# Moving six element-wise instructions on q from VectorE to GpSimd in an attention and MLP kernel

## The chip, the cores and the metric

The kernel runs on one core of one Trainium2 chip. The metric is the device time of one execution in microseconds (us). The kernel before takes 832.39 us, the median of 3 runs (832.22 to 834.11). The execution whose profile is read here took 833.08 us by itself; its span, from the first recorded instruction to the last, is 831.2 us.

## What is computed

Eight batches of linear attention, each with 8 heads, 576 positions and 64 features a head, feed a two-layer network:

```python
q_s = q - np.max(q, axis=-1, keepdims=True)
q_s = np.exp(q_s)
q_s = q_s / (np.sum(q_s, axis=-1, keepdims=True) + 1e-09)
k_s = k - np.max(k, axis=2, keepdims=True)
k_s = np.exp(k_s)
k_s = k_s / (np.sum(k_s, axis=2, keepdims=True) + 1e-09)
kv = np.einsum('bhsd,bhse->bhde', k_s, v)
x = np.einsum('bhsd,bhde->bhse', q_s, kv)      # then rows of 8 * 64 = 512
h = x @ w_in
sp = np.maximum(h, 0.0) + np.log1p(np.exp(-np.abs(h)))
out = (h * erf(sp)) @ w_out
```

The softmax of q is taken along the 64 features, that of k along the 576 positions. The change concerns two steps of the softmax of q: the subtraction of the maximum ahead of the exponential, and the multiplication by the reciprocal of the sum behind it.

## The kernel before, in words

**Attention.** A batch's q lies in SBUF as two tiles of 128 partitions x 1024 float32 values (`q_0` and `q_1` in the profile's and the order's names: half 0 and half 1 of the heads; 16 rows of 64 features in each partition). The last 64 positions of two batches share one tail tile of 128 x 512 (`qt`). k lies in two tiles of the same size and a tail `kt`. The function `attention(b)` emits the steps of one batch:

- `k_max` (lines 517, 518, 521) folds k to one row of maxima by `tensor_tensor` on VectorE, ending with the tail at L521. Four transposes on TensorE (`kT`, L528), a reduction on VectorE (`km`, L532) and four more transposes (`kB`, L543) bring the maxima back to all partitions, and L703 (twice) and L708 subtract them from k.
- `q_sub` takes the maxima of 16 rows (`tensor_reduce`, L464, into `q_m`, a tile with one buffer) and subtracts them (`tensor_tensor`, L465), in place.
- ScalarE takes the exponentials of k's and q's tiles (L348).
- `kv_mm` (L564) forms k times v on TensorE, `kv_norm` divides (L584 to L587).
- `q_norm` sums 16 rows (L471), adds and inverts (L473 or L475, L476) and multiplies in place (L478).
- q is then transposed on TensorE (`q_T`, L661; from batch 3 on by a DMA), copied by ScalarE (L651, L654), multiplied by kv (L679), and the product x is put into SBUF by ScalarE (L453). The PSUM tiles of q's transposes, of kT, kB, kv and of x share one pool of two banks (tag `bk`), so a transpose may have to wait until ScalarE has read an older tile.

**The network.** Tokens are cut into 12 blocks of 384, the hidden width into 4 groups of 512, which gives 48 steps n. Step n multiplies by w_in (`m`; L1036 in float32 for the first five steps, L997 in split float16 with one level of Strassen's scheme after that), takes softplus and erf on ScalarE (L348, with an activation table load ahead of each), multiplies on VectorE (L1074 or L1077), splits the result into two float16 parts (L1091, L1095) and multiplies by w_out (`M`; L1114 in float32, L1123 in float16). In the first 110 us VectorE also decodes the weights (three instructions for each piece: L213, L216, L219), and ScalarE squares them (L248) for a scale that `wscales` makes (from L257 on, with the transposes of L263 on TensorE and the reductions of L267 on VectorE). `wsplit` and `finish` split the weights and x into float16 parts (L299 on ScalarE, L300 on VectorE).

**Order.** The table ORDER and the function `pace` say in which order the steps are emitted. A list scheduler with its own cost estimates then sets the order on each engine; each engine runs its instructions strictly in that order. An instruction that is put on another engine therefore changes the order of others too. GpSimd's queue holds a few memsets (L443, L444), the loads of some weights (L187), and for batch 0 the subtraction of q's maxima (L857, four instructions of 128 x 512); SyncE's queue issues the other DMAs.

Of the kernel before, what the change touches and what calls it, by code (L numbers as in the profile page):

```python
# [55 lines left out]
def attn_moe_kernel(  # L56
# [9 lines left out]
    nc = tc.nc  # L66
# [276 lines left out]
    def act(out_, in_, func, chain=True, **kw):  # L343

        with ExitStack() as es:
            if chain and last[0] is not None:
                es.enter_context(tc.issue_after(last[0]))
            i = nc.scalar.activation(out_, in_, func, **kw)  # L348
        if chain:
            last[0] = i.ins  # L350
        return i
# [106 lines left out]
    def rows(t):  # L458
        return t.rearrange("p t h d -> p (t h) d")

    def q_sub(t, g, name):

        m = at.tile([P, g], F32, tag=f"qm{g}", bufs=1, name=f"{name}_m")
        nc.vector.tensor_reduce(m, t, axis=AX.X, op=ALU.max)  # L464
        nc.vector.tensor_tensor(  # L465
            t, t, m[:, :, None].to_broadcast([P, g, D]), op=ALU.subtract
        )

    def q_norm(t, g, name, b, o=None):
        r = at.tile([P, g], F32, tag=f"qr{g}", bufs=1, name=f"{name}_r")  # L470
        nc.vector.tensor_reduce(r, t, axis=AX.X, op=ALU.add)  # L471
        if b < E32:
            nc.vector.tensor_scalar_add(r, r, 1e-9)  # L473
        else:
            nc.vector.tensor_scalar(r, r, 1e-9, 2.0**-QS, op0=ALU.add, op1=ALU.mult)  # L475
        nc.vector.reciprocal(r, r)  # L476
        if o is None:
            nc.vector.tensor_tensor(  # L478
                t, t, r[:, :, None].to_broadcast([P, g, D]), op=ALU.mult
            )  # L480
            return
        for f in range(2):
            fs = slice(4 * f, 4 * f + 4)
            nc.vector.tensor_tensor(
                o[:, f * 2 * P:(f + 1) * 2 * P].rearrange("p (c a d) -> p a c d", c=2, a=2),
                t[:, fs].rearrange("p (a c) d -> p a c d", a=2),
                r[:, fs].rearrange("p (a c) -> p a c", a=2)[..., None].to_broadcast([P, 2, 2, D]),
                op=ALU.mult,
            )
# [22 lines left out]
    def k_max(b, ks, kt):  # L512

        kmax = asc[:, 0].rearrange("p (h d) -> p h d", h=H)
        k2 = asc[:, 1].rearrange("p (t h d) -> p t h d", t=2, h=4)
        for hf in range(2):
            nc.vector.tensor_tensor(k2, ks[hf][:, 0:2], ks[hf][:, 2:4], op=ALU.max)
            nc.vector.tensor_tensor(
                kmax[:, hf * 4:hf * 4 + 4, :], k2[:, 0], k2[:, 1], op=ALU.max
            )  # L520
        nc.vector.tensor_tensor(kmax[kt[1]], kmax[kt[1]], kt[0], op=ALU.max)  # L521
        return kmax

    def k_max_T(b, kmax):
        bk = bank(f"kT_{b}")
        km2 = hd(kmax)
        for c in range(NC4):
            nc.tensor.transpose(  # L528
                bk[:, c * P:(c + 1) * P], km2[:, c * P:(c + 1) * P], ident
            )  # L530
        km = at.tile([P, NC4], F32, tag="km", bufs=1, name=f"km_{b}")
        nc.vector.tensor_reduce(  # L532
            km, bk.rearrange("p (c s) -> p c s", c=NC4), axis=AX.X, op=ALU.max
        )
        return km
# [3 lines left out]
    def k_max_rows(b, km):  # L539

        bk = bank(f"kB_{b}")
        for c in range(NC4):
            kB[0] = nc.tensor.transpose(  # L543
                bk[:, c * P:(c + 1) * P], km[:, c:c + 1].to_broadcast([P, P]), ident
            )
        return bk.rearrange("p (h d) -> p h d", h=H)
# [97 lines left out]
    def q_turn_tail(p):  # L644
        t = q_turn(hd(bat[2 * p]["qt"]), asc[:, 0].bitcast(F16), 2)
        bat[2 * p]["qtT"] = t.rearrange("p (i c) s -> p i (c s)", i=2)
# [44 lines left out]
    def attention(b):  # L691
        d, j, p = bat[b], b % 2, b // 2
        even = bat[b - j]
        tl = slice(j * TAIL, (j + 1) * TAIL)
        ks, qs, kt = d["k"], d["q"], even["kt"][tl]
        kmax = k_max(b, ks, (kt, tl))
        yield SHARES[0]
        km = k_max_T(b, kmax)
        q_sub(rows(qs[0]), 16, f"q_{b}_0")
        yield SHARES[1]  # L700
        kb = k_max_rows(b, km)
        for hf in range(2):
            nc.vector.tensor_tensor(  # L703
                ks[hf], ks[hf],
                kb[:, None, hf * 4:hf * 4 + 4, :].to_broadcast([P, TM, 4, D]),
                op=ALU.subtract,
            )
        nc.vector.tensor_tensor(kt, kt, kb[tl], op=ALU.subtract)  # L708
        yield SHARES[2]
        q_sub(rows(qs[1]), 16, f"q_{b}_1")  # L710
        if j == 1:
            q_sub(even["qt"], H, f"qt_{p}")
        yield SHARES[3]
        for t in (*ks, kt, qs[0], qs[1], *([even["qt"]] if j == 1 else [])):
            act(t, t, AF.Exp, chain=b > 1)
        yield SHARES[4]
        kv_norm(b, 0, kv_mm(b, 0))
        if b > 1:
            d["v"].append(load_half(v, "v", b, 1))
        q_norm(rows(qs[0]), 16, f"q_{b}_0", b)  # L720
        yield SHARES[5]
        if b >= QDMA:
            q_turn_half(b, 0)
        kv_norm(b, 1, kv_mm(b, 1))
        if b + 1 < B:
            load_kv(b + 1)
        mx = kv_max(b)
        yield SHARES[6]
        kv_split(b, mx)
        yield SHARES[7]  # L730
        q_norm(rows(qs[1]), 16, f"q_{b}_1", b)
        if b >= QDMA:
            q_turn_half(b, 1)
        if j == 1:
            q_norm(even["qt"], H, f"qt_{p}", b, asc[:, 1] if b < QDMA else None)
            if b >= QDMA:
                q_turn_tail(p)
        yield SHARES[8]
        for i in ((3 * p + 1, 3 * p + 2) if j else (3 * p, 3 * p + 1)):
            while not x_free(i):  # L740
                yield 0

        def tails():
            if b < QDMA:
                bk = bank(f"qTt_{p}")
                for c in range(NC4):
                    nc.tensor.transpose(
                        bk[:, c * P:(c + 1) * P], asc[:, 1, c * P:(c + 1) * P], ident
                    )
                even["qtT"] = q_evac(b, 0, bk)  # L750
            yield SHARES[9]
            qT = even["qtT"]
            bks = [bank(f"xt_{p}_{a}") for a in range(2)]
            x = xblock(p * NBK + 1)
            for j_ in range(2):
                for hf in range(2):
                    oc = slice(hf * P + j_ * TAIL, hf * P + (j_ + 1) * TAIL)
                    qs_ = [
                        qT[:, :, (2 * hf + c) * P + j_ * TAIL:(2 * hf + c) * P + (j_ + 1) * TAIL]
                        for c in range(2)  # L760
                    ]
                    x_mm(2 * p + j_, hf, [bk[:, oc] for bk in bks], qs_)
            w = TAIL if b < E32 else P
            for a, bk in enumerate(bks):
                bk3 = bk[:, :2 * P].rearrange("p (f s) -> p f s", f=2)
                for j_ in range(P // w):
                    o = SM - T + j_ * TAIL
                    x_put(
                        bk3[:, :, j_ * TAIL:j_ * TAIL + w], x[:, a::2, o:o + w],
                        bat[j_]["sx"] if b < E32 else None,  # L770
                    )
            if b + 1 < B:
                bat[b + 1]["qt"] = load_tail(q, "qt", p + 1)
            yield SHARES[10]

        if j == 1 and b < QDMA:
            yield from tails()
        for hf in range(2):
            if hf == 1 and j == 1 and b >= QDMA:
                yield from tails()  # L780
            qTs = []
            for c in (2 * hf, 2 * hf + 1):
                qTs.append(q_T(b, c, bank(f"qT_{b}_{c}")) if b < QDMA else d["qT"][c])
                if b < QDMA and c % 2 == 1 and b + 1 < B:
                    load_q(b + 1, hf)
                yield SHARES[11]
            bks = [bank(f"x_{b}_{hf}_{a}") for a in range(2)]
            x_mm(b, hf, bks, qTs)
            if b >= QDMA and b + 1 < B:
                load_q(b + 1, hf)  # L790
            for a in range(2):
                x_split(b, 2 * hf + a, bks[a])
            if hf == 1:
                d["xdone"] = True
            yield 2 * SHARES[12]
# [480 lines left out]
```

## Time and profile before

| what | value |
|---|---|
| median of 3 runs | 832.39 us |
| the profiled execution | 833.08 us |
| its span | 831.2 us |
| TensorE busy | 804.8 us (97%) |
| VectorE busy | 626.6 us (75%) |
| ScalarE busy | 503.4 us (61%) |
| GpSimd busy | 15.9 us (2%), 37 instructions |
| granted TensorE clock | 1.0 |

The span is about 2 us below the time of the same execution; what lies around it is taken as unchanged. Busy time is a share of the whole span, and the kernel has stages: from about 40 us on TensorE has work nearly always; VectorE's busy tenths are 9 in ten of the first twelve of 40 equal slices (to about 250 us) and between 3 and 9 later. TensorE's busy time is a modelled one, so beside it the idle times that the view of waits lists are read: who waited, for which instruction, for how long in all, how often, and the longest.

### The profile page before, as it was taken

To read this page: it belongs to the slowest core of one execution; us is meant where nothing else is said; L and a number is where in the kernel's file an instruction comes from. 1 tells how busy PE (TensorE), PEld (TensorE's weight loads), DVE (VectorE), ACT (ScalarE), POOL (GpSimd) and SP (SyncE) were. 2 spreads that over 40 slices of the span, in tenths; PEclk is the share of its full clock that TensorE was granted. 3 is DMA by queue.
4 is the path that set the end of the run, shared out by engine and by line. 5 is a ranking of instruction groups with operands and counts; after the bars stand their busy time and mean duration, and the time that the engine had idled before them with its cause. 6 is when DMAs were issued, how large, how long until landed. Compare 5 with 4: busy or idle time off the path is not lost.

```text
span 831.2 us, 15665 instructions
## 1 busy us (share of the span) xinstructions
PE 804.8 (97%) x6610; PEld 546.8 (66%) x6610; DVE 626.6 (75%) x894; ACT 503.4 (61%) x644; POOL 15.9 (2%) x37
## 2 busy tenths in 40 slices
PE   5999999999999999999999999999999999999996
PEld 4555556666676667667767667767776777767762
DVE  6999899999997869757976779867875656544643
ACT  3697678886576656546744746645764555544442
POOL 2101000000000000000000000000000000000000
PEclk9999999999999999999999999999999999999999
DMA  9995721041146206111451205311220100100101
GB/s 248 409 227 181 194 51 39 2 108 40 51 71 140 77 6 137 56 26 27 100 123 39 64 1 109 89 27 27 65 51 15 39 1 2 39 1 2 39 1 39
DMA packets 141349, 61.56 MB, mean 74 GB/s; under 512 B 130528, under 2 KB 132576, under 8 KB 141280
## 3 DMA queue, kind: packets, MB, share of 16 engines
q1 hardware_dynamic: 139104, 52.18, 25.0%
q0 software_dynamic: 2176, 8.39, 2.8%
q8 instruction: 52, 0.85, 0.4%
q14 instruction: 17, 0.14, 0.1%
HBM read 45.09 MB, written 9.44 MB: 66 GB/s over the span
## 4 chain that ended last, share of the span: by engine, by line
PE 55%; DVE 27%; ACT 9%; issue 3%; DMA 3%; SPq 3%; POOL 0%; ACTq 0%; DVEq 0%; POOLq 0%
PE o L1123 27%; PE pX L997 13%; PE pZ L997 7%; DVE G L1077 3%; PE pY L997 3%; ACT G L348 3%; ACT L348 3%; DVE H L1095 3%; DVE wt L300 2%; SPq L419 2%; DVE x L300 2%; DMA q<-in_q_dram 2%; DVE H L1091 2%; DVE x L392 1%; PE x L679 1%
## 5 line engine op out<-in xcount | busy, mean ns | idle before, releaser
L1123 PE MATMUL o<-wt,H 128*128 128x512 f16 x1548 | 356.0, 379 | 1.7 <-DVE H L1091 1.3
L997 PEld LDWEIGHTS <-wt 128*128 128x128 f16 x3612 | 300.0, 98 | 36.5 <-issue 14.3
L1123 PEld LDWEIGHTS <-H 128*128 128x128 f16 x1548 | 149.2, 98 | 154.0 <-DVE H L1091 1.8
L997 PE MATMUL pX<-x,wt 128*128 128x192 f16 x2064 | 198.8, 246 | 3.8 <-DVE H L1019 2.4
L348 ACT ACT_TABLE_LOAD x104 | 133.4, 1283 | 7.0 <-DVE H L1022 5.2
L1077 DVE SCALAR_TENSOR_TENSOR G<-G,small,H 128x1536 f32<-128x1536 f32 x44 | 79.9, 1817 | 53.3 <-ACT G L348 53.0
L1024 ACT COPY H<-pX 128x384 f32<-128x384 f32 x43 | 20.4, 475 | 144.5 <-PE pX L997 141.4
L997 PE MATMUL pZ<-x,wt 128*128 128x192 f16 x1032 | 100.6, 246 | 0.0
L348 ACT ACTIVATE G<-H,U 128x768 f32<-128x768 f32 (+1 forms) x58 | 71.0, 1241 | 22.1 <-DVE H L1022 21.5
L1095 DVE TENSOR_TENSOR H<-G,H 128x1536 f16<-128x1536 f32 x43 | 75.5, 1755 | 0.8
L348 ACT ACTIVATE G<-G 128x1536 f32<-128x1536 f32 x48 | 71.3, 1485 | 0.5
L997 PE MATMUL pY<-x,wt 128*128 128x192 f16 x516 | 49.6, 246 | 0.3 <-DVE H L1009 0.3
L453 ACT ACTIVATE x<-x 128x384 f32<-128x384 f32 (+1 forms) x52 | 16.2, 397 | 48.4 <-PE x L679 48.4
L1022 DVE TENSOR_TENSOR H<-pZ,H 128x384 f32<-128x384 f32 x43 | 23.7, 551 | 26.2 <-PE pZ L997 26.2
L1009 DVE COPY H<-pY 128x384 f32<-128x384 f32 x43 | 23.8, 553 | 25.7 <-PE pY L997 25.7
L299 ACT ACTIVATE x<-x 128x768 f16<-128x768 f32 (+1 forms) x44 | 32.9, 765 | 15.2 <-DVE x L392 15.1
L1091 DVE CAST H<-G 128x1536 f16<-128x1536 f32 x43 | 41.1, 957 | 0.8
L300 DVE SCALAR_TENSOR_TENSOR x<-x,x 128x768 f16<-128x768 f32 (+1 forms) x44 | 37.3, 852 | 3.2 <-ACT x L299 3.2
L1139 DVE TENSOR_SCALAR ob<-o,V 128x512 f32<-128x512 f32 x29 | 21.7, 748 | 20.4 <-PE o L1123 20.4
L1011 DVE TENSOR_TENSOR H<-pX,H 128x384 f32<-128x384 f32 x43 | 23.9, 555 | 13.2 <-PE pX L997 12.4
L464 DVE TENSOR_REDUCE q_m<-q 128x16 f32<-128x1024 f32 x14 | 17.0, 1217 | 17.0 <-DMA q<-in_q_dram 16.8
L1036 PE MATMUL pX<-x,wt 128*128 128x384 f32 x80 | 28.3, 488 | 0.2 <-DVE wt L219 0.2
(183 smaller groups left out, 790.4 us busy)
## 6 DMA issues: line engine op xcount, KB each, us to landing
out_dram<-ob SPq DMA_DIRECT2D x32, 256.0 KB, 2.3
vbuf<-in_v_dram SPq DMA_DIRECT2D x56, 128.0 KB, 3.2
q<-in_q_dram SPq DMA_DIRECT2D x56, 128.0 KB, 3.2
k<-in_k_dram SPq DMA_DIRECT2D x56, 128.0 KB, 3.2
wt<-in_moe_w_out_dram POOLq DMA_DIRECT2D x5, 1024.0 KB, 6.6
wt<-in_moe_w_in_dram SPq DMA_DIRECT2D x4, 1024.0 KB, 11.9
wt<-in_moe_w_out_dram SPq DMA_DIRECT2D x2, 1024.0 KB, 15.5
H_raw<-in_k_dram SPq DMA_DIRECT2D x2, 512.0 KB, 4.8
```

Of the source, the lines that this page charges most:

```text
L299: nc.scalar.activation(hi, src, AF.Copy, scale=s)
L300: nc.vector.scalar_tensor_tensor(lo, src, s, hi, op0=ALU.mult, op1=ALU.subtract)
L348: i = nc.scalar.activation(out_, in_, func, **kw)
L997: nc.tensor.matmul(o, w[wl][:, c, a * P:(a + 1) * P], x[:, xl, xi, c, :], start=(new and a == 0 and c == 0 and i == 0), stop=(c == 1 and i ...
L1009: nc.vector.tensor_copy(C[0, 0], bank2("Y"))
L1011: add(C[0, 0], bank2("X"), C[0, 0], op=ALU.add)
L1022: add(C[0, 1], bank2("Z"), C[0, 1], op=ALU.add)
L1036: nc.tensor.matmul(ph[:, :T], w[:, c, a * P:(a + 1) * P], x[:, c, :], start=(c == 0), stop=(c == NC4 - 1),)
L1077: nc.vector.scalar_tensor_tensor(flat(s["G"]), flat(s["G"]), GA32 if n < N32 else GA[:, g:g + 1], flat(s["H"]), op0=ALU.mult, op1=ALU.mult,)
L1091: nc.vector.tensor_copy(flat(s["gh"]), flat(s["G"]))
L1095: nc.vector.tensor_tensor(flat(s["gl"]), flat(s["G"]), flat(s["gh"]), op=ALU.subtract)
L1123: nc.tensor.matmul(o, s[gt][:, a, ts_], w[wl][:, a, :], start=(first_ and a == 0 and i == 0), stop=(last_ and a == FG - 1 and i == 2),)
```

## The change

`q_sub` gets the batch as an argument and puts its `tensor_tensor` on GpSimd for batches below 3 (batch 0 does not come through `q_sub`, so these are 1 and 2; the call for the tail tile keeps VectorE). `q_norm` puts its `tensor_tensor` on GpSimd for batch 2, for the two full tiles. In all six instructions of 128 x 1024 float32 change their engine: four of L465 and two of L478.

```diff
-    def q_sub(t, g, name):
+    def q_sub(t, g, name, b=8):
         m = at.tile([P, g], F32, tag=f"qm{g}", bufs=1, name=f"{name}_m")
         nc.vector.tensor_reduce(m, t, axis=AX.X, op=ALU.max)
-        nc.vector.tensor_tensor(
+        (nc.gpsimd if b < 3 else nc.vector).tensor_tensor(
             t, t, m[:, :, None].to_broadcast([P, g, D]), op=ALU.subtract
         )
...
         if o is None:
-            nc.vector.tensor_tensor(
+            (nc.gpsimd if b == 2 else nc.vector).tensor_tensor(
                 t, t, r[:, :, None].to_broadcast([P, g, D]), op=ALU.mult
             )
             return
...
-        q_sub(rows(qs[0]), 16, f"q_{b}_0")
+        q_sub(rows(qs[0]), 16, f"q_{b}_0", b)
...
-        q_sub(rows(qs[1]), 16, f"q_{b}_1")
+        q_sub(rows(qs[1]), 16, f"q_{b}_1", b)
```

In GpSimd's queue the two subtractions of batch 1 stand ahead of the last five weight loads (L187); the two subtractions and the two multiplications of batch 2 stand behind the last of these loads, among the memsets of v's tail.

VectorE's queue in batch 1, around the maxima of k, before (wt_95 and wt_96 are weights that are decoded, asc holds the maxima of k, k_0, k_1 and kt_104 are k's tiles, q_0_235 is half 0 of q):

```order
L518 TENSOR_TENSOR asc<-asc 128x256
L216 SCALAR_TENSOR_TENSOR wt_95<-wt_89,wt_95 128x1024
L521 TENSOR_TENSOR asc<-asc,kt_104 64x512
L219 SCALAR_TENSOR_TENSOR wt_95<-wt_89,wt_95 128x1024
L532 TENSOR_REDUCE km_474<-kT_469 128x4
L471 TENSOR_REDUCE q_0_r<-q_0_235 128x16
L703 TENSOR_TENSOR k_0_352<-k_0_352,kB_479 128x1024
```

And VectorE's queue at the same place after the change:

```order
L471 TENSOR_REDUCE q_0_r<-q_0_235 128x16
L517 TENSOR_TENSOR asc<-k_1_357 128x512
L216 SCALAR_TENSOR_TENSOR wt_95<-wt_89,wt_95 128x1024
L518 TENSOR_TENSOR asc<-asc 128x256
L219 SCALAR_TENSOR_TENSOR wt_95<-wt_89,wt_95 128x1024
L521 TENSOR_TENSOR asc<-asc,kt_104 64x512
L473 TENSOR_SCALAR q_0_r<-q_0_r 128x16
L213 TENSOR_SCALAR wt_96<-wt_90 128x1024
L476 RECIPROCAL q_0_r<-q_0_r 128x16
L216 SCALAR_TENSOR_TENSOR wt_96<-wt_90,wt_96 128x1024
L532 TENSOR_REDUCE km_474<-kT_469 128x4
L478 TENSOR_TENSOR q_0_235<-q_0_235,q_0_r 128x1024
```

The sum L471 and the decode L219 now stand ahead of L521, and four instructions of the decode and of q's normalisation stand between L521 and the reduction L532.

ScalarE's queue in batch 2, ahead of the transposes of q's half 1 (wt_96 is the last weight that is split, H_1466 and G_1650 belong to a step of the network), as a difference:

```order
 L654 CAST asc<-qT_1_1600 128x512
+L299 ACTIVATE wt_96<-rw,small 128x2048
 L1024 COPY H_1466<-pX_1481 128x2x192
 L348 ACT_TABLE_LOAD
 L348 ACTIVATE G_1650<-H_1466,U_673 128x1536
-L299 ACTIVATE wt_96<-rw,small 128x2048
 L348 ACT_TABLE_LOAD
```

The split of the last weight now stands ahead of the copy and the softplus. On TensorE the transposes of q's half 1 of batch 2 (qT_2_1721; pZ_1728 is a product of the network's first layer) move at the same place:

```order
 L997 LDWEIGHTS wt_90
 L997 MATMUL pZ_1728<-x_2_1446,wt_90 128x192
+L661 MATMUL qT_2_1721<-ident,q_1_803 128x128 x4
 L997 LDWEIGHTS wt_90
 L997 MATMUL pZ_1728<-x_2_1446,wt_90 128x192
```

They stood behind all 12 products pZ_1728, the 12 products pX_1669 that follow, and the first product of L1123; they now stand behind 8 of the 12 products pZ_1728.

## The prediction

> **What bounds the kernel now.** I read the busy times first, then TensorE's waits in the stretch where the six instructions run, then the timeline of VectorE, ScalarE and TensorE at the places where TensorE waits.
>
> ```profile
> PE 804.8 (97%) x6610; PEld 546.8 (66%) x6610; DVE 626.6 (75%) x894; ACT 503.4 (61%) x644; POOL 15.9 (2%) x37
> ```
>
> TensorE (PE) is the bound; VectorE (DVE) is a quarter idle and GpSimd (POOL) almost wholly. Taking work off VectorE can only pay where TensorE stands still for VectorE, directly or through ScalarE. TensorE's waits from 45 to 250 us (waiting line, line waited for, us in all, times, longest):
>
> ```profile
> PE qT L661 <- ACT x L453: 1.9, 2, 1.4
> PE kT L528 <- DVE asc L521: 1.2, 1, 1.2
> PE kB L543 <- DVE km L532: 1.1, 1, 1.1
> PE kv L564 <- ACT k L348: 0.6, 1, 0.6
> PE pX L997 <- DVE H L1011: 0.5, 1, 0.5
> PE pY L997 <- DVE H L1009: 0.3, 1, 0.3
> ```
>
> These are 5.6 us together, 0.7% of the time. That is all that the change could win if every one of them went. A measurement of this kernel can tell about 0.3% from no change, 2.5 us.
>
> **What is removed and added.** The instructions of the two lines (minimum, median and maximum in ns):
>
> ```profile
> L465 DVE TENSOR_TENSOR q<-q,q_m x14: 1207/1222/1226, 52.2 to 570.9; 128x1024 f32<-128x1024 f32 x14
> L478 DVE TENSOR_TENSOR q<-q,q_r x16: 1211/1217/1227, 18.2 to 603.6; 128x1024 f32<-128x1024 f32 x16
> ```
>
> VectorE loses four of the first and two of the second, 7.3 us busy. In its queue one takes less, since the next starts ahead of its end: 53.29 - 52.15 = 1.14 us in the timeline below, 6.8 us for six. GpSimd does batch 0's subtraction already, in pairs of half the size (L857 below): a pair takes 2.06 us, so six instructions take 12.4 us on a queue that is almost idle, and each result comes 0.8 us later after its reduction, if nothing else holds GpSimd.
>
> Whether GpSimd and VectorE hold each other up is the unknown cost. The nearest rows are batch 0's, GpSimd subtracting with VectorE beside it:
>
> ```profile
> 15.36 1.21 DVE L843 TENSOR_TENSOR k<-H_raw,kB 128x1024 f32<-128x1024 f32 x1
> 15.52 2.06 POOL L857 TENSOR_TENSOR q<-G_raw,q_m 128x512 f32<-128x512 f32 x2 [1.33 <-DVE q_m L854]
> 16.49 1.21 DVE L471 TENSOR_REDUCE q_r<-q 128x16 f32<-128x1024 f32 x1
> ```
>
> Both VectorE instructions take 1.21 us, their usual time. But L843 has one operand in PSUM (kB) and L471 has one operand, while most of VectorE's queue in batches 1 and 2 reads two tiles from SBUF. So the price per instruction lies between 0 (as these rows) and 2.06 us of VectorE at a stand. I take 0, by the only rows in which the two engines work side by side, and keep 2.06 for the range and for the first rival. [...]
>
> **Place 1: batch 1's maxima of k, 50 to 75 us.** VectorE's queue, then TensorE's, then the first exponential of k:
>
> ```profile
> 52.15 1.22 DVE L465 TENSOR_TENSOR q<-q,q_m 128x1024 f32<-128x1024 f32 x1
> 53.29 1.23 DVE L219 SCALAR_TENSOR_TENSOR wt<-raw,wt 128x1024 int32<-128x1024 int32 x1
> ...
> 66.16 0.69 DVE L521 TENSOR_TENSOR asc<-asc,kt 64x512 f32<-64x512 f32 x1
> 66.88 1.23 DVE L219 SCALAR_TENSOR_TENSOR wt<-wt,wt 128x1024 int32<-128x1024 int32 x1
> 68.02 0.68 DVE L532 TENSOR_REDUCE km<-kT 128x4 f32<-128x512 f32 x1
> 68.62 1.21 DVE L471 TENSOR_REDUCE q_r<-q 128x16 f32<-128x1024 f32 x1
> 69.74 2.34 DVE L703 TENSOR_TENSOR k<-k,kB 128x1024 f32<-128x1024 f32 x2
> ...
> 72.84 0.17 DVE L473 TENSOR_SCALAR q_r<-q_r 128x16 f32<-128x16 f32 x1
> ...
> 74.79 1.22 DVE L478 TENSOR_TENSOR q<-q,q_r 128x1024 f32<-128x1024 f32 x1
> ```
> ```profile
> 66.90 0.66 PE L528 MATMUL kT<-ident,asc 128*128 128x128 f32 x4 [1.17 <-DVE asc L521]
> 67.40 1.46 PE L1036 MATMUL pX<-x,wt 128*128 128x384 f32 x4
> 68.76 0.65 PE L543 MATMUL kB<-ident,km 128*128 128x128 f32 x4
> ```
> ```profile
> 58.48 1.06 ACT L348 ACTIVATE q<-q 128x1024 f32<-128x1024 f32 x1 [0.81 <-DVE q L465]
> ...
> 74.68 2.01 ACT L348 ACTIVATE k<-k 128x1024 f32<-128x1024 f32 x2
> ```
>
> Two subtractions leave ahead of L521, 2 x 1.14 = 2.28 us. The new order fills the room: L219 (68.02 - 66.88 = 1.14) and L471 (69.74 - 68.62 = 1.12) now stand ahead of L521. So L521 stays at 66.16, and TensorE's wait of 1.17 us for it stays: no gain. Behind L521, L532 now follows L473, L213, L476 and L216, 74.79 - 72.84 = 1.95 us, in place of L219's 1.14, so km is made 0.8 us later, from 68.8 to 69.5 by L532's 0.68. TensorE covers most of that with one more matrix product of pX (two of them took 68.76 - 67.40 = 1.36 us): it comes to kB at 69.4 and waits about 0.15 us. Without that cover it would be the whole 0.8. L478 delays L703 by 1.14 more: it starts at 71.7 and is through both tiles at 71.7 + 2.34 = 74.0; ScalarE starts on them at 74.68, held by its own softplus ahead: no cost. **+0.15 us.**
>
> On GpSimd the subtractions are queued ahead of weight loads. Those wait for decodes that now come earlier, and GpSimd is idle meanwhile: nothing. The exponential of q's half 1 waits 0.81 us for L465 today; in the new queue one L465 less stands ahead of its maximum, and L1074, which stood between the two, does not, so that GpSimd's longer time is covered. The tile q_m has one buffer, so VectorE's maximum of half 1 now waits until GpSimd has read that of half 0; between the two stand L216, L213 and L219, over 2 x 1.14 = 2.28 us of work against GpSimd's 2.06, so no wait, and one of what is missing if GpSimd starts late, with all of VectorE's queue behind it. Behind that exponential on ScalarE stand three squares and the copies of pX and pY; on the copy of pX waits TensorE's fourth product, whose bank it frees.
>
> **Place 2: the scale of the weights and the first split products, 108 to 138 us.**
>
> ```profile
> 111.34 0.60 PE L263 MATMUL ws_out<-ident,small 128*128 128x128 f32 x4
> ```
> ```profile
> 112.36 0.68 DVE L267 TENSOR_REDUCE wse_in<-ws_in 128x4 f32<-128x512 f32 x1
> ...
> 130.74 1.81 DVE L1077 SCALAR_TENSOR_TENSOR G<-G,small,H 128x1536 f32<-128x1536 f32 x1
> ...
> 135.40 0.55 DVE L1009 COPY H<-pY 128x384 f32<-128x384 f32 x1
> ...
> 137.06 0.55 DVE L1011 TENSOR_TENSOR H<-pX,H 128x384 f32<-128x384 f32 x1
> ```
>
> L267 started 1.0 us after TensorE had gone on from ws_in to ws_out; VectorE was behind with L465 and the folds of k. Without L465 it starts up to 0.9 us sooner, and the second L465, which stood ahead of L1077, saves another 1.14, of which two folds of k that moved in take most. L1009 and L1011 come about 1 us sooner, and TensorE's waits for them, 0.3 + 0.5 us, go; next late is the split of x on ScalarE and VectorE, which moves with them. **-0.8 us**; between 0 and -0.8. In batch 1's tail, around 100 us, two blocks of products change places with a copy of ScalarE; two products moved ahead fill that time, and I count nothing.
>
> **Place 3: the transposes of q's half 1, 180 to 206 us.**
>
> ```profile
> 194.82 1.28 DVE L300 SCALAR_TENSOR_TENSOR wt<-wt,small,wt 128x1024 f16<-128x1024 f32 x1
> ```
> ```profile
> 194.99 1.28 ACT L348 ACT_TABLE_LOAD   x1 [0.38 <-DVE H L1022]
> ...
> 197.76 1.99 ACT L299 ACTIVATE wt<-rw,small 128x2048 f16<-128x2048 f32 x1
> ...
> 202.45 1.19 ACT L453 ACTIVATE x<-x 128x384 f32<-128x384 f32 x4
> ```
> ```profile
> 199.36 1.16 PE L997 MATMUL pZ<-x,wt 128*128 128x192 f16 x12
> 200.36 1.15 PE L997 MATMUL pX<-x,wt 128*128 128x192 f16 x12
> ...
> 203.14 0.66 PE L661 MATMUL qT<-ident,q 128*128 128x128 f32 x4 [1.41 <-ACT x L453]
> 203.64 2.54 PE L1123 MATMUL o<-wt,H 128*128 128x512 f16 x11
> 206.01 0.60 PE L661 MATMUL qT<-ident,q 128*128 128x128 f32 x4
> ```
>
> L299 may overwrite wt_96 only when VectorE's last read of it, the L300 that ends at 194.82 + 1.28 = 196.1, is over. Two L478 less, it ends at 193.8. ScalarE then does L299 (2.0), the copy of pX (about 0.4, an estimate) and the rest of the chain to L453 (202.45 - 194.99 less L299's 1.99 = 5.47): L453 starts at 201.7, 0.8 us sooner. But TensorE now asks for the bank after 8 of the 12 products pZ, at 199.36 + 8/12 = 200.0, and gets it 0.69 us after L453's start as today, at 202.4: a wait of 2.3 us in place of 1.41. Then come the transposes (0.5), 4 products pZ, 12 pX and 12 of L1123 (0.33 + 1.0 + 2.6 at the rows' pace) ahead of the next transposes, which start at 206.8 in place of 206.01. **+0.8 us**; between 0 and 0.8, since a chain that ends sooner gives it back.
>
> **Sum:** 0.15 - 0.8 + 0.8 = 0.15 us, 0.2 rounded. From the profiled execution's 833.08 that is 833.3; this execution lies 0.7 above the median of the runs, so 832.6 for the median. The waits of 0.6 us for k's exponential and of 1.1 us for km in a later batch hang on ScalarE and on queues that the change leaves as they are.
>
> **Rivals.** *VectorE stands still while GpSimd reads.* For it: the instructions around are mostly ones with two SBUF operands, and a stand of GpSimd's 2.06 us is longer than the 1.14 that VectorE is spared. Against it: the rows of batch 0 show no delay. Place 1 decides: two such stands put L521, and with it kT, up to 2 x 2.06 = 4.1 us later, about 4.0 with a little of it beside one-operand reductions, and nothing else is queued that TensorE may do first. At place 2 the gain is lost. At place 3 the two stands put VectorE's L300, and with it L299, L453 and the transposes, about as much later again: 0.8 + 4.0. Sum 0.15 + 4.0 + 4.8 = 9.0 us: 841.4. It decides from about 0.6 us of stand per instruction: four of them, at places 1 and 3, make 2.4 us. [...]
>
> *VectorE's relief reaches TensorE.* If the waits for L521, km, L1009, L1011 and k's exponential all go (1.2 + 1.1 + 0.5 + 0.3 + 0.6 = 3.7 us): 828.7. For it: all hang on a VectorE queue that has hardly a gap there. Against it: at place 1 the order fills the room again, and at place 3 it asks for the bank sooner.
>
> **How the numbers follow.** No change that can be told: 0.43, with a range of its own of 830 to 835. The stand: 0.38. The relief: 0.15. 0.04 is for a swap that costs over 2.5 us elsewhere. So faster 0.15, same 0.43, slower 0.42. The range reaches up to nine tenths of the stand and down to three quarters of the relief: 829.6 to 840.5.
>
> **What would show it.** VectorE's two-operand instructions beside GpSimd's (L216, L219, L517, L1077) keep their 1.2, 0.7 and 1.8 us, and no gap opens; GpSimd's take about 2.1; L521 in batch 1 within 0.5 us of 66.2; kT's wait about 1.2; no wait for L1009 and L1011 near 136; the transposes' wait near 202 about 2.3. Wrong is the forecast if L521 comes at 68 or later, or VectorE's instructions stretch.

## The result and the profile after

The kernel after takes 841.55 us, the median of 4 runs (840.28 to 842.33), against 833.25 us for the kernel before beside it (832.22 to 834.9, 4 runs). The ratio is 1.0095, 95% interval 1.0076 to 1.0114: slower by about 8 us, a little above the range of the prediction and at the time of its first rival. The profiled execution took 842.33 us, its span is 840.5 us, 9.3 more than before.

The busy times of the page of after:

```profile
PE 807.7 (96%) x6610; PEld 549.2 (65%) x6610; DVE 627.3 (75%) x888; ACT 503.7 (60%) x644; POOL 35.3 (4%) x43
```

VectorE lost six instructions, 6.8 us of its queue by the forecast, and is yet busy for 0.7 us longer than before: what it was spared came back as longer instructions. GpSimd gained 19.4 us for six instructions, 3.2 each, where 2.06 was counted. The timeline of GpSimd in after (start, duration, what ended the idle time before):

```profile
50.49 2.66 POOL L465 TENSOR_TENSOR q<-q,q_m 128x1024 f32<-128x1024 f32 x1 [15.08 <-DVE q_m L464]
56.23 4.35 POOL L465 TENSOR_TENSOR q<-q,q_m 128x1024 f32<-128x1024 f32 x1 [3.09 <-DMA k<-in_k_dram]
...
133.15 6.20 POOL L465 TENSOR_TENSOR q<-q,q_m 128x1024 f32<-128x1024 f32 x1 [18.81 <-ACT wt L299]
...
188.18 2.12 POOL L478 TENSOR_TENSOR q<-q,q_r 128x1024 f32<-128x1024 f32 x1 [3.42 <-DVE q_r L476]
```

Now the timeline of VectorE in after, at the three places:

```profile
51.30 2.40 DVE L213 TENSOR_SCALAR wt<-rw 128x1024 int32<-128x1024 int32 x1
...
54.81 1.20 DVE L464 TENSOR_REDUCE q_m<-q 128x16 f32<-128x1024 f32 x1
...
59.34 2.35 DVE L219 SCALAR_TENSOR_TENSOR wt<-rw,wt 128x1024 int32<-128x1024 int32 x1
...
68.17 0.69 DVE L521 TENSOR_TENSOR asc<-asc,kt 64x512 f32<-64x512 f32 x1
...
137.52 0.54 DVE L1009 COPY H<-pY 128x384 f32<-128x384 f32 x1
137.99 2.45 DVE L300 SCALAR_TENSOR_TENSOR wt<-wt,small,wt 128x1024 f16<-128x1024 f32 x1
...
184.63 1.22 DVE L471 TENSOR_REDUCE q_r<-q 128x16 f32<-128x1024 f32 x1 [0.97 <-POOL q L478]
...
187.92 3.66 DVE L326 TENSOR_TENSOR wt<-wt 128x512 f32<-128x512 f32 x3
...
199.05 2.47 DVE L300 SCALAR_TENSOR_TENSOR wt<-wt,small,wt 128x1024 f16<-128x1024 f32 x2
```

Two instructions that lie side by side here are both long. L213 takes 2.40 us, where it takes 0.68 in before, beside GpSimd's 2.66; L219 takes 2.35 in place of 1.23 while GpSimd's second subtraction is under way, and that one takes 4.35. The reduction at 54.81, with one operand, keeps its 1.20. From 133.15 GpSimd stands for some four microseconds (6.20 us in place of 1.90) under L1077 and the two-operand instructions that follow it without a gap and keep their times (1.80 us, then L300's 1.27 and 1.81 for two; 1.81, 1.28 and 1.82 in before). It ends at 139.35; less 1.90, that puts the point at which it gets in at about 137.45, beside L1009 at 137.52, whose operand is in PSUM, and then L300 is the one that stretches (2.45 us in place of 1.27). L521 comes at 68.17, 2.0 us later than before. VectorE's work on this batch begins with the maximum L464, which waits for q's transfer: it starts at 49.88 in the execution of before and at 49.03 in that of after. From L464's start to L521's it is 16.28 us before and 19.14 after, 2.9 more. TensorE's waits in after from 45 to 250 us:

```profile
PE kT L528 <- DVE asc L521: 3.2, 1, 3.2
PE pX L997 <- ACT H L1024: 2.7, 1, 2.7
PE pX L997 <- DVE H L1011: 2.2, 1, 2.2
```

The wait for L521 grew from 1.2 to 3.2, that for L1011 from 0.5 to 2.2, and a wait of 2.7 for ScalarE's copy L1024 is new. ScalarE's timeline in after ahead of that copy:

```profile
201.62 2.00 ACT L299 ACTIVATE wt<-rw,small 128x2048 f16<-128x2048 f32 x1 [2.84 <-DVE wt L300]
203.53 0.46 ACT L1024 COPY H<-pX 128x384 f32<-128x384 f32 x1
```

The copy stands behind the split L299, which the new order moved ahead of it, and L299 has waited 2.84 us for VectorE's L300, the pair that ends at 199.05 + 2.47 = 201.5. Before, L300 ended at 196.1: that is 5.4 us later, in a kernel whose TensorE is 5.5 us late there by then. So against the kernel's own lateness L300 is where it was, and the 2.3 us that it should have come sooner by the forecast are gone.

The waits alone are not all. TensorE's timeline in after behind the wait for L521:

```profile
68.91 0.66 PE L528 MATMUL kT<-ident,asc 128*128 128x128 f32 x4 [3.23 <-DVE asc L521]
69.40 3.42 PE L1036 MATMUL pX<-x,wt 128*128 128x384 f32 x6
72.61 1.01 PE L543 MATMUL kB<-ident,km 128*128 128x128 f32 x4
73.46 2.74 PE L1114 MATMUL o<-wt,G 128*128 128x512 f32 x6
```

And the table of the stretches of 2 us there (busy times by engine; the granted clock is the third number from the end):

```profile
70.00:72.00 2.00, 2.00 (x5) 1.04 (x4) 2.00 (x3) 0.00 (x0) 0.00 (x0) 0.51 0.80 260
72.00:74.00 2.00, 2.00 (x8) 1.35 (x7) 0.98 (x2) 1.12 (x2) 0.00 (x0) 0.64 0.61 248
74.00:76.00 2.00, 2.00 (x6) 0.85 (x5) 2.00 (x2) 1.99 (x2) 0.00 (x0) 1.00 0.00 0
```

The six records of pX (a float32 product shows as two, as in the kernel for the clock below, x80 for 40) take 3.42 us; before, four took 1.46, so six would take about 2.1. The granted clock is 0.51 from 70 to 72 us, and the 0.64 of the next row, read as half clock and then full, is a half clock up to about 73.4: by an estimate from these two rows, some 3.4 us at half clock. The transposes start 2.0 us late (68.91 against 66.90), the L1114 behind them 3.6 us late (73.46 against 69.89), 1.6 more.

### The profile page after: what moved, and what is told of

The parts are those of the page before. It is cut to its first block, busy times and chain, and to the rows that moved or that the text cites. A ratio compares the mean times of both kernels' runs of the same rounds, so it can differ in the third digit from the quotient of the medians.

```text
span 840.5 us, 15677 instructions
## 1 busy us (share of the span) xinstructions
PE 807.7 (96%) x6610; PEld 549.2 (65%) x6610; DVE 627.3 (75%) x888; ACT 503.7 (60%) x644; POOL 35.3 (4%) x43
## 4 chain that ended last, share of the span: by engine, by line
PE 64%; DVE 18%; ACT 9%; DMA 3%; issue 3%; SPq 3%; POOL 1%; ACTq 0%; DVEq 0%; POOLq 0%
PE o L1123 28%; PE pX L997 15%; PE pZ L997 7%; PE pY L997 3%; ACT L348 3%; ACT G L348 3%; PE o L1114 3%; DVE G L1077 3%; DVE H L1095 2%; SPq L419 2%; PE pX L1036 2%; PE kv L564 2%; DVE x L300 1%; DVE H L1091 1%; PE x L679 1%
## 5 line engine op out<-in xcount | busy, mean ns | idle before, releaser
L1123 PE MATMUL o<-wt,H 128*128 128x512 f16 x1548 | 355.8, 379 | 1.7 <-DVE H L1091 1.3
L1123 PEld LDWEIGHTS <-H 128*128 128x128 f16 x1548 | 149.1, 98 | 154.2 <-DVE H L1091 1.8
L1077 DVE SCALAR_TENSOR_TENSOR G<-G,small,H 128x1536 f32<-128x1536 f32 x44 | 79.9, 1816 | 53.8 <-ACT G L348 53.7
L1024 ACT COPY H<-pX 128x384 f32<-128x384 f32 x43 | 20.4, 475 | 145.2 <-PE pX L997 145.2
L348 ACT ACTIVATE G<-H,U 128x768 f32<-128x768 f32 (+1 forms) x58 | 71.0, 1241 | 22.1 <-DVE H L1022 21.5
L1095 DVE TENSOR_TENSOR H<-G,H 128x1536 f16<-128x1536 f32 x43 | 75.4, 1754 | 0.9
L348 ACT ACTIVATE G<-G 128x1536 f32<-128x1536 f32 x48 | 71.2, 1484 | 0.5
L453 ACT ACTIVATE x<-x 128x384 f32<-128x384 f32 (+1 forms) x52 | 16.2, 397 | 48.5 <-PE x L679 48.5
L1022 DVE TENSOR_TENSOR H<-pZ,H 128x384 f32<-128x384 f32 x43 | 23.7, 551 | 26.3 <-PE pZ L997 26.2
L1009 DVE COPY H<-pY 128x384 f32<-128x384 f32 x43 | 23.8, 553 | 25.3 <-PE pY L997 25.3
L299 ACT ACTIVATE x<-x 128x768 f16<-128x768 f32 (+1 forms) x44 | 32.9, 765 | 16.1 <-DVE x L392 16.0
L300 DVE SCALAR_TENSOR_TENSOR x<-x,x 128x768 f16<-128x768 f32 (+1 forms) x44 | 37.2, 849 | 3.2 <-ACT x L299 3.2
L1011 DVE TENSOR_TENSOR H<-pX,H 128x384 f32<-128x384 f32 x43 | 23.8, 554 | 13.7 <-PE pX L997 12.8
L464 DVE TENSOR_REDUCE q_m<-q 128x16 f32<-128x1024 f32 x14 | 17.0, 1215 | 17.9 <-DMA q<-in_q_dram 17.9
```

The lines of the kernel that those rows point to most:

```text
L299: nc.scalar.activation(hi, src, AF.Copy, scale=s)
L300: nc.vector.scalar_tensor_tensor(lo, src, s, hi, op0=ALU.mult, op1=ALU.subtract)
L1009: nc.vector.tensor_copy(C[0, 0], bank2("Y"))
L1011: add(C[0, 0], bank2("X"), C[0, 0], op=ALU.add)
L1077: nc.vector.scalar_tensor_tensor(flat(s["G"]), flat(s["G"]), GA32 if n < N32 else GA[:, g:g + 1], flat(s["H"]), op0=ALU.mult, op1=ALU.mult,)
L1095: nc.vector.tensor_tensor(flat(s["gl"]), flat(s["G"]), flat(s["gh"]), op=ALU.subtract)
```

## The experiments

Theory A, a supposition to be tested: where VectorE's instruction has two operands in SBUF, it and GpSimd's stand still for each other. Theory B: the time goes with the changed order on TensorE, VectorE and ScalarE, whoever does the six instructions.

**The two engines alone.** Eight VectorE instructions of one kind, beside four subtractions of 128 x 1024 on GpSimd or none; nothing of the kernel's work is done.

```diff
+    def pool_tt():
+        for _ in range(4):
+            nc.gpsimd.tensor_tensor(c, c, m[:, :, None].to_broadcast([P, 16, 64]), op=ALU.subtract)
+    def v_two():
+        for _ in range(8):
+            nc.vector.tensor_tensor(h, a, b, op=ALU.subtract)
...
+    for vec, pool in (
+        (v_two, None), (None, pool_tt), (v_two, pool_tt), (v_sum, pool_tt),
+        (v_psum, pool_tt), (v_scalar, pool_tt), (v_two, pool_set), (v_scalar, None),
+    ):
```

> This kernel leaves out the whole computation: it runs stages of VectorE instructions of 128 x 1024 values alone, GpSimd's tensor_tensor alone, and both side by side, each stage behind a fence of ScalarE copies. Theory A (VectorE stands still while GpSimd reads): beside GpSimd the subtraction of two SBUF tiles and the integer tensor_scalar lose up to 2.06 us per GpSimd instruction, or GpSimd is the one that waits; tensor_reduce (1.2 us) and the subtraction with a PSUM operand keep their time, and memsets on GpSimd cost the subtraction nothing. Theory B (the new order of the queues costs the time): every duration is the same alone and side by side, 1.2 us for VectorE's and 2.06 us for GpSimd's instructions.

VectorE's timeline in this kernel (L70 reads two SBUF tiles, L74 one, L78 one and PSUM, L82 is a shift with one operand like L213):

```profile
9.19 10.04 DVE L70 TENSOR_TENSOR h<-a,b 128x1024 f32<-128x1024 f32 x8 [9.19 <-ACT a L57]
35.95 16.36 DVE L70 TENSOR_TENSOR h<-a,b 128x1024 f32<-128x1024 f32 x8 [16.72 <-ACT a L57]
56.92 10.00 DVE L74 TENSOR_REDUCE rd<-a 128x16 f32<-128x1024 f32 x8 [4.60 <-ACT a L57]
70.50 11.51 DVE L78 TENSOR_TENSOR h<-a,pt 128x512 f32<-128x512 f32 x16 [3.58 <-ACT a L57]
86.61 12.10 DVE L82 TENSOR_SCALAR h<-a 128x1024 int32<-128x1024 int32 x8 [4.60 <-ACT a L57]
103.32 10.04 DVE L70 TENSOR_TENSOR h<-a,b 128x1024 f32<-128x1024 f32 x8 [4.60 <-ACT a L57]
118.27 5.79 DVE L82 TENSOR_SCALAR h<-a 128x1024 int32<-128x1024 int32 x8 [4.91 <-ACT a L57]
```

And GpSimd's:

```profile
24.88 7.84 POOL L62 TENSOR_TENSOR c<-c,m 128x1024 f32<-128x1024 f32 x4 [24.44 <-ACT m L58]
36.30 11.15 POOL L62 TENSOR_TENSOR c<-c,m 128x1024 f32<-128x1024 f32 x4 [3.59 <-ACT m L58]
58.08 7.84 POOL L62 TENSOR_TENSOR c<-c,m 128x1024 f32<-128x1024 f32 x4 [10.62 <-ACT m L58]
...
86.96 9.03 POOL L62 TENSOR_TENSOR c<-c,m 128x1024 f32<-128x1024 f32 x4 [8.27 <-ACT m L58]
103.41 8.02 POOL L66 MEMSET c<- 128x1024 f32 x8 [7.42 <-ACT a L57]
```

Eight two-operand instructions take 10.04 us alone and 16.36 beside four of GpSimd's: (16.36 - 10.04) / 4 = 1.58 us for each of GpSimd's. The shift pays the same price, (12.10 - 5.79) / 4 = 1.58, although it has one operand; why it does, no run shows. Reductions and instructions with an operand in PSUM pay nothing here: the eight reductions take 1.22 us each on the mean, as in the kernel before, and the sixteen subtractions from PSUM 0.69, as L517 of the same size does in before. GpSimd keeps 7.84 us for four beside both, as alone, and its memsets cost VectorE nothing (10.04 us for eight beside them, as alone). The price is less than the whole of GpSimd's 7.84 / 4 = 1.96 us.

**Left out.** The six instructions are done by nobody, so that the softmax of q in batches 1 and 2 lacks them; TensorE's order is that of after.

```diff
-        (nc.gpsimd if b < 3 else nc.vector).tensor_tensor(
+        if b < 3:
+            return
+        nc.vector.tensor_tensor(
...
-            (nc.gpsimd if b == 2 else nc.vector).tensor_tensor(
+            if b == 2:
+                return
+            nc.vector.tensor_tensor(
```

> This kernel leaves out the six instructions (four subtractions of q's maxima, two multiplications by the reciprocal sums): neither VectorE nor GpSimd does them. TensorE's order is that of the changed kernel. Theory A (VectorE stands still while GpSimd reads): the order alone costs next to nothing, 830 to 834 us. Theory B (the new order of the queues costs the time): about 841 us, as the changed kernel.

It took 831.59 us against 833.19: ratio 0.9983, interval 0.9973 to 0.9993. TensorE's wait for the copy L1024 is 0.9 us there, where it is 2.7 in after. So the order of after costs nothing as long as VectorE is not late, and theory B falls. It is also about the most that the idea could bring in this order, with GpSimd's work for free: 0.2%.

**Added.** The kernel before, where VectorE keeps its six instructions; GpSimd does as many on a spare tile, at the same places, in halves of 128 x 512.

```diff
+        if b < 3:
+            for i in range(0, g, 8):
+                nc.gpsimd.tensor_tensor(
+                    dum, dum, m[:, i:i + 8, None].to_broadcast([P, 8, D]), op=ALU.subtract
+                )
         nc.vector.tensor_tensor(
             t, t, m[:, :, None].to_broadcast([P, g, D]), op=ALU.subtract
         )
```

> The kernel before, with its order on TensorE, VectorE and ScalarE, and six times two GpSimd tensor_tensor of 128 x 512 on a spare tile beside it, at the places of the six instructions, reading the same maxima and sums; VectorE still does its own six. Theory A (VectorE stands still while GpSimd reads): slower than before by 4 to 12 us, since VectorE loses up to 2.06 us for each pair and is spared nothing. Theory B (the new order of the queues costs the time): the same as before within 0.3%.

It took 842.22 us, ratio 1.0104 (1.0086 to 1.0122), with the orders of before and work that nobody waits for. GpSimd's work beside VectorE is enough for the loss. TensorE's waits in this kernel from 45 to 250 us (the added lines shift the numbers: L540 and L533 are L528 and L521, L673 and L455 are L661 and L453):

```profile
PE kT L540 <- DVE asc L533: 3.3, 1, 3.3
PE qT L673 <- ACT x L455: 3.1, 2, 2.6
```

**Place 3 in the old order.** After, with the split L299 of the last weight held behind the softplus, where it stood before; TensorE's transposes stand there as before, too.

```diff
-            split2(stg.pop(jn), whalf(jn, 0), whalf(jn, 1), s)
+            with tc.issue_after(soft[0].ins) if jn == NJ - 1 else ExitStack():
+                split2(stg.pop(jn), whalf(jn, 0), whalf(jn, 1), s)
```

> The changed kernel with one more rule for the order: the split of the last weight on ScalarE stays behind the softplus, as before the change. If the changed kernel's loss around 200 us (3.2 us more lag of TensorE) comes from that split standing ahead of the copy that frees pX's bank: 2.5 to 3.5 us faster than the changed kernel, 838 to 839 us. If it comes from VectorE's lateness alone: within 1 us of the changed kernel's 841.5.

840.65 us, ratio 1.0084 (1.0069 to 1.01). That is 0.9 us less than after, whose interval overlaps: the two are not told apart, as expected if the loss comes from VectorE's lateness. TensorE's wait at place 3 in this kernel, and the row of ScalarE that it goes back to (numbers are shifted by one: L662, L349 and L1023 are L661, L348 and L1022):

```profile
PE qT L662 <- issue: 3.0, 1, 3.0
```
```profile
201.21 1.28 ACT L349 ACT_TABLE_LOAD   x1 [1.94 <-DVE H L1023]
```

The wait for L1024 is gone, and one of 3.0 us for the transposes of q has come in its place. The view of waits names no releaser for it. ScalarE's chain to the copy that frees the transposes' bank begins at 201.21, after a wait of 1.94 us for VectorE's L1022, where it was 0.38 before; the copy starts at 208.68 and the transposes 0.74 us behind that, as they start 0.69 behind it in before. So place 3 loses by VectorE's lateness in the old order, too, and the order decides where it shows.

**One place at a time.** Batch 1's subtractions alone, batch 2's alone, and batch 2's multiplications alone on GpSimd (the line of the condition is `b == 1`, `b == 2`, or the subtraction stays on VectorE):

```diff
-        (nc.gpsimd if b < 3 else nc.vector).tensor_tensor(
+        (nc.gpsimd if b == 1 else nc.vector).tensor_tensor(
...
-            (nc.gpsimd if b == 2 else nc.vector).tensor_tensor(
+            nc.vector.tensor_tensor(
```

> Only batch 1's two subtractions go to GpSimd. Theory A (VectorE stands still while GpSimd reads two SBUF operands, and the three places add): only place 1's loss, 2 to 3.5 us over before, 835 to 837, with kT's wait near 3 us and the products behind it at half clock, and no wait for L1009 or L1011 near 138. Rival (one lateness is enough: the queues behind place 1 turn it into the whole loss): 840 to 842.

> Only batch 2's two subtractions go to GpSimd; the order at place 1 is that of before. Theory A: only place 2's loss, 2 to 4 us over before, 835 to 837.5, with L1009 and L1011 late near 138 and kT's wait of batch 1 at 1.2 us. Rival (GpSimd starved there for 4 us has room, since place 2 had slack in the forecast): within 1 us of before.

> Only batch 2's two multiplications go to GpSimd; place 3 has the changed order. Theory A: only place 3's loss, 3 to 4.5 us over before, 836 to 837.5, with the transposes of q's half 1 or the copy ahead of them late near 200. If the places add, the losses of these three kernels sum to the whole change's 8 to 9 us. Rival (the late x of place 3 was inherited from places 1 and 2): within 1.5 us of before.

| kernel | median, us | ratio (95%) | span of the profiled execution, over before's 831.2 |
|---|---|---|---|
| batch 1's subtractions | 837.38 | 1.0075 (1.0052 to 1.0098) | 834.4, +3.2 |
| batch 2's subtractions | 834.84 | 1.0031 (1.002 to 1.0041) | 834.2, +3.0 |
| batch 2's multiplications | 835.86 | 1.0048 (1.003 to 1.0066) | 834.3, +3.1 |
| all six (after) | 841.55 | 1.0095 (1.0076 to 1.0114) | 840.5, +9.3 |

The kernel before beside the first three took 832.1. The medians lie up to 0.4 us outside the ranges expected by theory A (835 to 837, 835 to 837.5, 836 to 837.5) and further from those of the rivals. Each place loses by itself, so none inherits its whole loss. By the profiled spans the three add up to the whole, 9.3, but these are single executions; by the medians they come to 1.54% against 0.95%, more than the whole. One thing that does not add up is seen in the profiled executions: each of the three kernels has a stretch of half clock at its own place (0.53 from 70 to 72 us, 0.57 from 138 to 140, 0.50 from 200 to 202), while after has them at places 1 and 2 and keeps 1.00 behind its wait of 2.7 us at place 3. What else the places take from each other stays open. For batch 2's subtractions the profiled execution, 836.02 us, is 1.2 above the median, and seven of the ten executions have a mean clock of 1.0, so the half clock at this place does not come each time. TensorE's order near 140 us in this kernel is in part neither that of before nor that of after, so some of its loss can be the order's.

For place 2, VectorE's timeline in the kernel with batch 2's subtractions alone:

```profile
130.28 3.36 DVE L1077 SCALAR_TENSOR_TENSOR G<-G,small,H 128x1536 f32<-128x1536 f32 x1
```

GpSimd's, and TensorE's behind it:

```profile
130.13 1.90 POOL L465 TENSOR_TENSOR q<-q,q_m 128x1024 f32<-128x1024 f32 x1 [19.05 <-DVE q_m L464]
```
```profile
135.76 1.07 PE L997 MATMUL pZ<-x,wt 128*128 128x192 f16 x11 [0.97 <-DVE x L300]
138.29 2.08 PE L997 MATMUL pY<-x,wt 128*128 128x192 f16 x12 [1.46 <-DVE H L1009]
```

GpSimd came at 130.13 here, ahead of L1077 and not behind it as in after: L1077 takes 3.36 in place of 1.81, and GpSimd its undisturbed 1.90. It came 0.15 us ahead of L1077 here (130.13 and 130.28) and 0.29 us behind it in after (133.15 and 132.86). The products behind the second wait take 2.08 us for twelve where 1.15 is usual: the half clock again (0.57 from 138 to 140 us).

**Quarters.** After, with each of GpSimd's instructions cut into four.

```diff
+        n = 4 if b < 3 else g
+        for i in range(0, g, n):
+            (nc.gpsimd if b < 3 else nc.vector).tensor_tensor(
+                t[:, i:i + n], t[:, i:i + n],
+                m[:, i:i + n, None].to_broadcast([P, n, D]), op=ALU.subtract
+            )
```

> The whole change, with each of the six GpSimd instructions cut into four of 128 x 256. If the stand is set by the time for which GpSimd reads, whatever its pieces, VectorE stands as long in all: 840 to 843, with VectorE's instructions stretched by about 0.5 us each, and more of them. If VectorE's instructions with a PSUM operand or with one operand fill the room between pieces, part comes back: 836 to 840. If each change of hands costs something by itself, it is slower than the change: over 843.

837.91 us, ratio 1.0068 (1.0055 to 1.008): the second case, part comes back, though the interval just touches that of after (1.0076 to 1.0114). GpSimd's timeline in this kernel:

```profile
132.79 12.16 POOL L467 TENSOR_TENSOR q<-q,q_m 128x256 f32<-128x256 f32 x4 [17.78 <-ACT wt L299]
```

At place 2 the four pieces took 12.16 us, and L1077's and L300's instructions beside them kept their 1.80 and 1.27: here GpSimd stood and VectorE did not, and no wait of TensorE for that q is listed. At place 1 L213 took 1.10 us in place of 0.68 and L219 1.65 in place of 1.23: a piece that had got in held VectorE for 0.4 us, where the long instruction held it for 1.1 to 1.7. The kernel is still slower than before.

**Later batches.** Six subtractions on GpSimd, but those of batches 4 to 6; TensorE's and ScalarE's orders are those of before.

```diff
-        (nc.gpsimd if b < 3 else nc.vector).tensor_tensor(
+        (nc.gpsimd if 4 <= b < 7 else nc.vector).tensor_tensor(
...
-            (nc.gpsimd if b == 2 else nc.vector).tensor_tensor(
+            nc.vector.tensor_tensor(
```

> Six subtractions of the same size go to GpSimd, but those of batches 4, 5 and 6, where VectorE is busy for 34 to 42 us of each 50 before; TensorE's and ScalarE's order stays that of before, and VectorE's but for a few rows. Theory A with slack: VectorE's neighbours are stretched in the same way (two-operand instructions to 2 to 3 us), but VectorE has the room, so the time is within 2 us of before, 831 to 834. Rival (a stand of VectorE costs TensorE wherever it falls): about 9 us more, 840 to 842.

834.22 us against 832.74, ratio 1.0018 (1.0003 to 1.0033). The stretch is there as well, as in VectorE's timeline in this kernel:

```profile
380.99 2.26 DVE L300 SCALAR_TENSOR_TENSOR x<-x,x 128x384 f16<-128x384 f32 x1
...
389.15 1.75 DVE L1095 TENSOR_TENSOR H<-G,H 128x1536 f16<-128x1536 f32 x1
390.82 0.55 DVE L1019 TENSOR_TENSOR H<-pX,H 128x384 f32<-128x384 f32 x1
```

And in before:

```profile
387.37 0.55 DVE L1019 TENSOR_TENSOR H<-pX,H 128x384 f32<-128x384 f32 x1
387.84 1.75 DVE L1095 TENSOR_TENSOR H<-G,H 128x1536 f16<-128x1536 f32 x1
```

L1077 at 479.56 took 3.31 us, 1.5 more than its 1.81, and no wait of TensorE grew by it: the one for L1019 near it is 0.6 us, where it is 0.9 in before. L300 took 2.26 us, 1.7 more than its 0.56 in before. In this stretch TensorE waited; its waits in this kernel from 380 to 430 us:

```profile
PE pX L997 <- DVE H L1019: 2.5, 1, 2.5
```

But this wait is not the stand's. L1019 came 3.45 us later than in before, and VectorE's order is not that of before here: L1095 and an L300 now stand ahead of L1019 and take 2.54 us of the 3.45. L300's stretch less the L465 that VectorE is spared makes 0.6, and a later transfer of q 0.3. Without the new order L1019 would have ended at 388.8, just as TensorE came for it. So with room in VectorE's queue the loss is a fifth of the change's, and no stand is shown to cost TensorE anything there. It is not a gain either.

**The clock.** TensorE does runs of 40 float32 products of 128 x 384 with waits of four lengths between, and nothing of the kernel's work. Each product shows as two records (x80 for 40 below).

```diff
+    for rep in range(3):
+        for n in (1, 2, 3, 4):
+            for i in range(40):
+                nc.tensor.matmul(pt[:, :384], a[:, :128], h[:, :384], start=True, stop=True)
+            nc.vector.tensor_copy(c[:, 0:384], pt[:, :384])
+            for _ in range(n):
+                nc.vector.tensor_reduce(
+                    a[:, 0:16], src.rearrange("p (r d) -> p r d", r=16), axis=AX.X, op=ALU.max)
```

> The whole computation is left out. TensorE does 40 float32 products of 128 x 384 in a row, then stands still for about 2, 3, 4.2 and 5.4 us (a chain of VectorE instructions of 1.2 us), three times over. If a wait alone halves the granted clock behind it, the products behind waits of about 3 us and more take about 0.65 us each in place of 0.32 for some microseconds, and those behind the shortest waits do not. If the half clock behind place 1 came from something else there (transfers, the weights' loads), all products take 0.32 us.

TensorE's timeline in this kernel:

```profile
36.73 26.04 PE L47 MATMUL p<-h,a 128*128 128x384 f32 x80 [1.87 <-DVE a L50]
65.89 27.73 PE L47 MATMUL p<-h,a 128*128 128x384 f32 x80 [3.12 <-DVE a L50]
97.99 28.86 PE L47 MATMUL p<-h,a 128*128 128x384 f32 x80 [4.38 <-DVE a L50]
132.49 28.68 PE L47 MATMUL p<-h,a 128*128 128x384 f32 x80 [5.63 <-DVE a L50]
```

And its stretches behind the second of these waits:

```profile
66.00:68.00 2.00, 2.00 (x4) 1.14 (x5) 0.00 (x0) 0.00 (x0) 0.00 (x0) 0.54 0.00 0
68.00:70.00 2.00, 2.00 (x5) 0.97 (x5) 0.00 (x0) 0.00 (x0) 0.00 (x0) 0.61 0.00 0
70.00:72.00 2.00, 2.00 (x8) 1.21 (x7) 0.00 (x0) 0.00 (x0) 0.00 (x0) 1.00 0.00 0
```

Behind a wait of 1.87 us the run takes 26.04, with the clock at 1.00 from 36 to 44 us; behind 3.12 it takes 27.73, 1.7 more, with the clock at half up to about 69.6 us (0.54 and 0.61 in the first two stretches), some 3.4 us at half clock; behind 4.38 and 5.63 it takes 2.8 and 2.6 more. There the clock is at half up to about 103.7 and 137.8 us (0.50 from 98 to 102 and 0.57 from 102 to 104; 0.50 from 132 to 136 and 0.54 from 136 to 138). A wait alone did it here. The three repeats give the same figures to 0.02 us.

## Why the prediction was wrong

**What bounds the kernel.** Right: TensorE's waits below 250 us were the whole of what could be won, 5.6 us, and with the instructions gone altogether 1.6 us were had.

**The price of a GpSimd instruction.** This is the step that failed: "I take 0, by the only rows in which the two engines work side by side". Those rows held a reduction and an instruction with a PSUM operand, and the two engines alone show that just these kinds paid nothing (1.22 and 0.69 us each), while the two-operand instruction and the shift, the kinds around the change, paid 1.58 us, between the bounds of 0 and 2.06 and far above the 0.6 at which the rival decided. The text had noticed that the rows were of the wrong kind, and used them for the value all the same. In after, five VectorE instructions are longer, by 1.7, 1.1, 0.9, 1.2 and 1.6 us (L213, L219, L517, L300 and L326), and L471 waits 1.0 us for GpSimd: 7.5 us, 1.2 to 1.3 for each of the six, where each spares it 1.14.

**Place 1.** Forecast +0.15, rival +4.0. L213 stretched by 1.7 us and L219 by 1.1, 2.8 together; VectorE had started on q's maxima 0.85 us sooner (49.03 in after, 49.88 before, when q's transfer let it), so L521 came 2.0 late. With that came the forecast's own sign of being wrong, L521 at 68 or later. That the wait for it stays at 1.2 was wrong. That GpSimd's longer time is covered for the exponential of q's half 1 was wrong, too: ScalarE waited 3.6 us for it, in place of 0.81, though no wait of TensorE behind that is listed. That "nothing else is queued that TensorE may do first" was right. What nobody had priced is the half clock: 1.6 us more by the L1114 behind. By 110 us some of it is given back: the same products run 2.25 us late there.

**Place 2.** Forecast -0.8, and 0 with the rival. TensorE's lag grows there from 2.25 to 5.3 us, 3.1 in place of 0 or less: the rival let the gain go, and did not count that L300, or L1077, stretches ahead of L1009 and L1011, for which TensorE waits. Batch 2's subtractions alone lose 3.0 by the spans, with the half clock in it. In after it is in this, too: the stretch from 142 to 144 us in after has a granted clock of 0.50, behind the wait of 2.2.

**Place 3.** Forecast +0.8, rival +4.8; the lag grows by 3.2, from 5.5 to 8.7 us. L326 (3.66 us for three, in place of 1.9) and a wait of VectorE for GpSimd's multiplication made VectorE late as the rival said, but the place where it shows was another: the copy L1024 (0.46 us in after and 0.48 in before, where the forecast had estimated 0.4) behind the split L299, not the transposes.

**The sum.** The rival's 9.0 stands beside 8.3 by the medians and 9.3 by the spans of the profiled executions. In these TensorE's lag is made of 2.3, 3.1 and 3.2 us at the three places, where the rival had 4.15, 0 and 4.8, and of 0.9 late in the kernel, where TensorE waits 1.4 us in place of 0.5 for a copy of ScalarE. That VectorE stands beside GpSimd was right (1.58 us for each of GpSimd's instructions in the two engines alone); that its sum is close is luck, since it lacked the half clock and had the places' sizes wrong. The chance of 0.38 for it was too small: nothing in the trace spoke against it for two-operand instructions.

**The relief and the order.** The part of the forecast that is left when the stand is taken out, +0.15, is measured by the kernel without the six: 1.6 us faster than before. That the new order fills the room ahead of L521 was right: from L464's start to L521's it is 16.25 us there and 16.28 in before. L521 came at 65.13, 1.0 sooner, only because q's transfer let L464 start at 48.88. It moves as much where the order is that of before: with batch 2's subtractions alone L521 came at 64.99, with its multiplications alone at 66.36, and TensorE waited 0.3 and 1.9 us for it. So before's wait of 1.17 us, which the forecast took as given, is partly the moment at which q arrives. Where the 1.6 us come from is not settled.

## What to carry to other kernels

Before work goes from VectorE to GpSimd, look at what stands in VectorE's queue beside it: two-operand and shift instructions on SBUF paid 0.9 to 1.7 us here for a 128 x 1024 instruction of GpSimd, about as much as VectorE is spared or more; reductions (1.22 us) and instructions with a PSUM operand (0.69) paid nothing. A row in which two engines do not disturb each other proves something only for the kinds of instruction in it; where the rows are of the wrong kind, price the unknown from its upper bound. And a wait of TensorE of 3.1 us cost 1.7 us more than its length in the kernel for the clock, by a half clock behind it. Before a wait of one profile is counted as a gain or a loss, look at what set its start: here the wait for L521 was 0.3 us in one execution and 1.9 in another, by the arrival of a transfer.

## What was not expected of the hardware

- In the kernel for the clock, the granted clock fell to half for some 3.4 us behind a wait of 3.1 us (0.54 from 66 to 68 us and 0.61 from 68 to 70), and not behind one of 1.9 (1.00 from 36 to 44). The way back took 3.4 us behind the wait of 3.1 us and 5.7 and 5.4 us of the run behind the longer ones, where the clock reads 0.50. Shorter waits came ahead of a half clock as well: in the kernel with batch 2's subtractions alone it was two of 1.0 and 1.5 us with 1.07 us of work between them (0.57 from 138 to 140). The length alone does not decide: a wait of 2.7 us did it in the kernel with batch 2's multiplications alone (clock 0.50 from 200 to 202 us) and one of 2.7 us did not in after (1.00 from 204 to 206).
- The stand goes both ways, and unevenly: GpSimd got in between VectorE's two-operand instructions one by one in the test of the two engines alone (11.15 us for its four, in place of 7.84), yet stood for over 4 us at 133 us in after (6.20 us in place of 1.90) while VectorE went on without a gap, and for most of 12.16 us in quarters. What decides this turn is not settled. Instructions behind each other in VectorE's queue were of several kinds there and of one kind in the test. In the test the reductions start 1.25 us apart, (10.00 - 1.22) / 7, and take 1.22; in the kernel the next starts ahead of the other's end (1.14 and 1.22).
- Side by side, four of GpSimd's instructions cost VectorE 1.58 us each, less than the 1.96 us that one takes alone (7.84 / 4): by an estimate from the two, about 0.4 us of it runs beside VectorE's.
